# Loading four token tiles, a three-row rotation table and a last tile stored in two pieces: one change to a fused S5 and GEGLU kernel

## The chip, the cores and the metric

The kernel runs on one core of one Trainium2 chip. Its time is the device time of a whole execution in microseconds (us), the median of three runs; lower is better. A profiled execution gives besides the span, which is the stretch from the first to the last recorded instruction, and the time of each instruction in it.

## The reference

Input x is one sequence of 2048 tokens with 512 features, in bf16. The output is x plus the product of two branches of its layer norm:

```python
xn  = layernorm(x)                                    # 2048 x 512
Lam_bar = exp(dt * Lam);  B_bar = ((Lam_bar - 1) / Lam)[:, None] * B   # complex, 512 states
h_t = Lam_bar * h_(t-1) + B_bar @ xn_t                # over all 2048 tokens
s   = 2 * real(h @ C.T) + xn * Dskip
g   = silu((gelu(xn @ w_gate) * (xn @ w_up)) @ w_down)  # 512 -> 1376 -> 512
out = x + s * g
```

## The kernel before

**Tiling.** The 2048 tokens are four slabs of 512, and a slab is four row tiles of 128 tokens. Per slab the kernel normalises x, transposes it (`xnT`), multiplies it with the gate and up weights (1376 columns in chunks of 512, 512 and 352), multiplies the two results (`gated`), transposes that product by DMA (`at_t`, L549) and multiplies it with the down weight (`down_pair`, L562). Beside it, `half(s, h)` multiplies the slab with B for half of the states (L613), copies the result to a buffer `U` (L615), rotates it back by the angle of each token so that the complex recurrence becomes a real one, scans it (L644) and rotates it forward into `hst`. `y_part` (L573 to L587) multiplies `hst` with C (L577), starting from the skip term that ScalarE writes to the PSUM bank (L573), multiplies by the gate branch (L583), adds x (L584) and stores.

**The rotation.** `turn` multiplies `U` (or the scan's result `Fs`) with the tables in one instruction of 4096 elements per partition (`rot`, L625) into `Q`, and adds the two halves of `Q` (L637). The tables `tab` hold four rows: cosine, cosine again, sine and minus sine. The second cosine is copied by two DMAs, the last row by ScalarE. In slab 0 only rows 0 and 2 are read.

**The start of slab 0.** There is no transposed input yet, so TensorE transposes the tiles itself: `center(m)` subtracts the mean of tile m (ScalarE's sum at L421, VectorE's subtraction at L422), `head_t(m)` transposes it into a bank (L385, L398) and VectorE copies it out (L400) to `xcT`. The up weights come row tile by row tile (128 of the 512 features each), and `up_rows(m, k, c)` is one matmul of 512 columns for token tile m, weight row tile k and chunk c (L460), so that work can begin before all rows are there. Chunk 2 of up (352 columns) and all of gate follow by `first_w` (L497). Only then do slab 1 and later slabs go through `gate_tile` (L534), with `xnT` written by a DMA transpose (`dma_t4`, L434).

**What sets the order.** Each piece of work is a step in a plan: its engine, a function that emits it, what it reads and writes. `Plan.run` emits the steps in the order of a long tuple `ORDER`, written out as numbers. `SLOTS` says in the same way which buffer each group of a rotating pool takes, and `SIZES` how many the pool has: `ps` (six PSUM banks), `pp` (two), `U` and so on. So each engine does its steps in the order in which they stand in `ORDER`, and waits by semaphores. The cost and due-time arguments of the steps play no part at run time. All large transfers are issued from one queue, SP's; three small loads of parameters are issued by ScalarE's. The steps are numbered as they are created, and a step added early shifts all later numbers.

The emitted queue of SP begins: token tiles 0, 1 and 2 of slab 0; chunk 0 and chunk 1 of up row 0; up rows 1 and 2; token tile 3; up row 3; the last 352 columns of up; columns 512 to 1375 of gate; its first 512 columns; slab 1; `Drow`; then the DMA transposes of slab 0 and of B.

Of the kernel before, what the change touches and what calls it, by code (L numbers as in the profile page):

```python
# [10 lines left out]
AF = mybir.ActivationFunctionType  # L11
ALU = mybir.AluOpType
# [39 lines left out]
    ),  # L52
    "pp": (
        0, 0, 1, 0, 1, 0, 0, 1, 0, 1, 1, 0, 0, 0, 1, 0, 1, 0, 1, 0, 1, 1, 0, 1, 0, 1, 0, 0, 1, 0, 1, 0, 1, 1, 0, 0, 0, 1, 1,
    ),
    "U": (
        1, 0, 2, 1, 0, 2, 1, 0,
    ),
    "g2": (
        2, 1, 0, 5, 4, 2, 0, 3, 1, 0, 5, 3, 4, 2, 1, 5,  # L60
    ),
    "at": (
        3, 0, 2, 1, 3, 1, 2, 0, 0, 3, 2, 1, 2, 0, 1, 0,
    ),
    "gtA": (
        0, 1, 1, 0, 0, 0, 1, 1, 1, 1, 0, 1, 0, 1, 0, 1,
    ),
    "gtB": (
        0, 0, 1, 1, 1, 0, 1, 0, 0, 0, 1, 0, 0, 0, 1, 0,
    ),  # L70
    "ubA": (
        0, 0, 1, 1, 1, 0, 1, 0, 0, 1, 0, 1,
    ),
    "ubB": (
        1, 0, 1, 1, 0, 0, 1, 0, 0, 1, 0, 1,
    ),
    "yg": (
        0, 1, 0, 0, 1, 1, 1, 1, 0, 1, 0, 0, 1, 0, 1, 1, 1, 0,
    ),
    "ot": (  # L80
        0, 0, 1, 1, 1, 1, 0, 1, 1, 0, 0, 0, 1, 0, 1, 1, 0,
    ),
    "sk": (
        1, 0, 3, 2, 6, 4, 7, 5, 3, 2, 1, 0, 4, 7, 6, 5,
    ),
    "atT": (
        1, 0, 2, 3, 1, 2, 0, 2, 1, 3, 3, 2, 1, 0, 0, 2,
# [4 lines left out]
SIZES = {"ps": 6, "pp": 2, "U": 3, "g2": 6, "at": 4, "gtA": 2, "gtB": 2, "ubA": 2, "ubB": 2, "yg": 2, "ot": 2, "sk": 8, "atT": 4}  # L92
# [56 lines left out]
def kernel(  # L149
# [17 lines left out]
    nc = tc.nc  # L167
# [28 lines left out]
    def sb(name, shape, dt=BF16):  # L196
        return consts.tile(shape, dt, name=name)
# [20 lines left out]
    NU = 3  # L218
# [5 lines left out]
    tab = sb("tab", [P, 4, NPT, TS])  # L224
# [28 lines left out]
    def dve(n, emit, reads=(), writes=(), rate=1.0, base=DV, **kw):  # L253
        return pl.add(DVE, base + n / 960.0 / rate, emit, reads, writes, lag=0.13, **kw)
# [312 lines left out]
    def y_part(s, m, c0, c1):  # L567
# [7 lines left out]
        def f():  # L575
# [6 lines left out]
        go, io = pl.group("ot")  # L582
        dve(w, lambda: V.tensor_tensor(out=yg[iy][:, 0:w], in0=ps, in1=g2[ig][:, c0:c1], op=ALU.mult), [key, ("g2", gg)], [("yg", gy)])  # L583
        dve(w, lambda: V.tensor_tensor(out=ot[io][:, 0:w], in0=yg[iy][:, 0:w], in1=x_tok[:, s * M + m, c0:c1], op=ALU.add),  # L584
            [("yg", gy), ("x", s, m)], [("ot", go)], rate=2.0)
        mg = s * TS + m * P
        dma(SP, 0.35, 1.5, lambda: nc.sync.dma_start(out=out_td[mg : mg + P, c0:c1], in_=ot[io][:, 0:w]), [("ot", go)], [("out", s, m, c0)], svc=(2, 0.4, 0.9))  # L587

    def y_tile(s, m):
        cuts = (0, HD, D) if (s, m) == (NS - 1, M - 1) else (0, D)  # L590
        for c0, c1 in zip(cuts, cuts[1:]):
            y_part(s, m, c0, c1)
# [8 lines left out]
    TABS = ["tab0", "tab10", "tab11", "tab2", "tab3"]  # L601
    CTS = [("CT", 0), ("CT", 1)]

    def half(s, h):
# [17 lines left out]
        tf = tab[:, :, hs, :].rearrange("p (j r) q t -> p j r (q t)", j=2)  # L622
# [5 lines left out]
        def turn(src, dst, reads, writes, back):  # L628
            if s == 0:
                rot(src, tf[:, :, 0, :].unsqueeze(2).to_broadcast(WQ), reads + ["tab0", "tab2"])  # L630
                for ri in range(2):
                    op = ALU.add if (ri == 0) == back else ALU.subtract
                    dve(1024, lambda ri=ri, op=op: V.tensor_tensor(out=dst[:, ri, :], in0=Qf[:, 0, ri, :], in1=Qf[:, 1, 1 - ri, :], op=op),
                        ["Q"], writes, rate=2.0)
            else:
                rot(src, tf[:, :, ::-1, :] if back else tf, reads + TABS)
                dve(2048, lambda: V.tensor_tensor(out=dst, in0=Qf[:, 0, :, :], in1=Qf[:, 1, ::-1, :], op=ALU.add), ["Q"], writes, rate=2.0)  # L637
# [51 lines left out]
    def tables():  # L689
# [19 lines left out]
        tt(tab[:, 0], t1, t2, ALU.subtract, ["Q1", "Q2"], ["tab0"])  # L709
        tt(v4(t1), highs[1], lows[0], ALU.mult, ["sp", "ch"], ["Q1"])  # L710
        tt(v4(t2), highs[0], lows[1], ALU.mult, ["cp", "sh"], ["Q2"])
        tt(tab[:, 2], t1, t2, ALU.add, ["Q1", "Q2"], ["tab2", "Q"])
        for h in range(2):
            hp = slice(h * H2, (h + 1) * H2)
            dma(SP, 0.5, 2.0, lambda hp=hp: nc.sync.dma_start(out=tab[:, 1, hp, :], in_=tab[:, 0, hp, :]), ["tab0"], [f"tab1{h}"], svc=(2, 0.8, 1.0))
        acts(2048, lambda: act(out=tab[:, 3], in_=tab[:, 2], func=AF.Copy, scale=-1.0), ["tab2"], ["tab3"])
# [203 lines left out]
```

## Time and profile before

| | |
|---|---|
| three runs, median (lowest to highest) | 178.75 us (178.42 to 178.96) |
| the profiled execution's own time | 179.15 us |
| its span | 177.3 us |
| granted TensorE clock | 1.00 |
| instructions | 2411 |
| TensorE (PE) busy | 172.1 us, 97% |
| VectorE (DVE) busy | 155.6 us, 88% |
| ScalarE (ACT) busy | 131.4 us, 74% |
| GpSimd (POOL) busy | 11.9 us, 7% |

The page is one profiled execution. In its rows a group of instructions stands as engine, line of the kernel, operation, output <- input, with the shape of one and how many there are; x17 means 17 of them. A timeline row starts with the start and the length in microseconds, counted from the start of the span; what stands in brackets at its end is idle time before it and what ended it. The chain of waits follows the work that ended last back through what released each step. PE busy is the time in which TensorE has a matmul, and PEld its weight loads, which overlap it. Queue rows (SPq) show when the issuing engine wrote a transfer's descriptors, not when the data moved; the time to landing is in the DMA view.

### The profile page before, as it was taken

To read this page: it belongs to the slowest core of one execution; us is meant where nothing else is said; L and a number is where in the kernel's file an instruction comes from. 1 tells how busy PE (TensorE), PEld (TensorE's weight loads), DVE (VectorE), ACT (ScalarE), POOL (GpSimd) and SP (SyncE) were. 2 spreads that over 40 slices of the span, in tenths; PEclk is the share of its full clock that TensorE was granted. 3 is DMA by queue.
4 is the path that set the end of the run, shared out by engine and by line. 5 is a ranking of instruction groups with operands and counts; after the bars stand their busy time and mean duration, and the time that the engine had idled before them with its cause. 6 is when DMAs were issued, how large, how long until landed. Compare 5 with 4: busy or idle time off the path is not lost.

```text
span 177.3 us, 2411 instructions
## 1 busy us (share of the span) xinstructions
PE 172.1 (97%) x834; PEld 82.2 (46%) x849; DVE 155.6 (88%) x253; ACT 131.4 (74%) x245; POOL 11.9 (7%) x25
## 2 busy tenths in 40 slices
PE   8999999999999999999999999999999999999992
PEld 2455444454544444444454545454444444444451
DVE  3745799999889999899999999999999998999343
ACT  6779999989999999994749854685577866159210
POOL 1553300000002001300000000000000000000000
PEclk9999999999999999999999999999999999999999
DMA  5999999999914400600450431800500940320421
GB/s 153 286 357 228 149 255 215 274 234 234 201 37 81 81 0 4 118 0 0 77 117 4 89 90 59 163 0 4 111 0 0 204 99 4 73 67 30 83 89 59
DMA packets 48467, 19.19 MB, mean 108 GB/s; under 512 B 40296, under 2 KB 47816, under 8 KB 48456
## 3 DMA queue, kind: packets, MB, share of 16 engines
q1 hardware_dynamic: 48432, 19.04, 48.8%
q8 instruction: 6, 0.10, 0.2%
q14 instruction: 5, 0.04, 0.1%
q10 hardware_dynamic: 24, 0.00, 0.0%
HBM read 6.46 MB, written 2.10 MB: 48 GB/s over the span
## 4 chain that ended last, share of the span: by engine, by line
PE 80%; DMA 12%; ACT 3%; SPq 2%; issue 1%; DVE 0%; ACTq 0%
PE bank L534 31%; PE bank L562 21%; PE bank L577 16%; PE bank L613 12%; DMA xnT<-xna 7%; DMA x_tok<-in_A_x_dram 5%; ACT xna L843 2%; SPq L287 1%; ACT gtA L503 1%; ACT at L469 1%; SPq L296 1%; DVE yg L583 0%; DVE ot L584 0%; ACT gtB L503 0%; ACTq L843 0%
## 5 line engine op out<-in xcount | busy, mean ns | idle before, releaser
L534 PEld LDWEIGHTS <-xnT 128*128 128x128 bf16 x288 | 28.1, 98 | 29.5 <-DMA xnT<-xna 0.6
L562 PE MATMUL bank<-wd,atT 128*128 128x512 bf16 (+1 forms) x171 | 39.4, 379 | 0.3
L534 PE MATMUL bank<-wu,xnT 128*128 128x512 bf16 (+1 forms) x142 | 32.5, 357 | 0.1
L534 PE MATMUL bank<-wg,xnT 128*128 128x512 bf16 (+1 forms) x139 | 31.7, 356 | 0.4
L613 PE MATMUL bank<-xnT,BT 128*128 128x512 bf16 x128 | 31.7, 379 | 0.0
L644 DVE TENSOR_TENSOR_SCAN Fs<-rho,ini,W 128x512 bf16<-128x512 f32 x24 | 29.9, 1272 | 0.1
L577 PE MATMUL bank<-C,hst 128*128 128x512 bf16 (+1 forms) x135 | 29.1, 367 | 0.1
L562 PEld LDWEIGHTS <-atT 128*128 128x128 bf16 (+1 forms) x176 | 17.2, 98 | 20.4
L615 ACT ACTIVATE U<-bank 128x512 bf16<-128x512 f32 x32 | 18.5, 611 | 6.3 <-PE bank L613 6.3
L565 ACT ACTIVATE g<-bank 128x512 f32<-128x512 f32 x16 | 9.5, 596 | 14.7 <-PE bank L562 14.6
L537 ACT ACTIVATE ubA<-bank 128x512 bf16<-128x512 f32 x24 | 14.6, 609 | 7.4 <-PE bank L534 5.4
L577 PEld LDWEIGHTS <-hst 128*128 128x128 bf16 x136 | 13.3, 98 | 14.2
L613 PEld LDWEIGHTS <-BT 128*128 128x128 bf16 x128 | 12.4, 98 | 14.4 <-DMA BT<-in_A_B_re_dram 0.4
L625 DVE TENSOR_TENSOR Q<-U,tab 128x4096 bf16<-128x4096 bf16 x8 | 18.3, 2290 | 0.5
L625 DVE TENSOR_TENSOR Q<-Fs,tab 128x4096 bf16<-128x4096 bf16 x8 | 18.3, 2289 | 0.2
L583 DVE TENSOR_TENSOR yg<-bank,g 128x512 bf16<-128x512 f32 (+1 forms) x17 | 11.0, 656 | 7.1 <-PE bank L577 6.6
L537 ACT ACTIVATE gtA<-bank 128x512 bf16<-128x512 f32 x24 | 14.5, 609 | 1.8 <-PE bank L534 1.5
L838 ACT ACTIVATE junk<-x_tok 128x512 bf16<-128x512 bf16 x16 | 10.3, 660 | 0.0
L573 ACT ACTIVATE bank<-sk 128x512 f32<-128x512 bf16 (+1 forms) x17 | 9.9, 590 | 0.1
L497 PE MATMUL bank<-wg,W 128*128 128x512 bf16 (+1 forms) x47 | 9.9, 357 | 0.1
L644 DVE TENSOR_TENSOR_SCAN Fs<-rho,W 128x512 bf16<-128x512 f32 x8 | 9.5, 1211 | 0.0
L843 ACT ACTIVATE xna<-x_tok,nb,rs 128x512 bf16<-128x512 bf16 x12 | 9.3, 826 | 0.0
(120 smaller groups left out, 185.1 us busy)
## 6 DMA issues: line engine op xcount, KB each, us to landing
out_dram<-ot SPq DMA_DIRECT2D x15, 128.0 KB, 1.7
x_tok<-in_A_x_dram SPq DMA_DIRECT2D x3, 512.0 KB, 6.2
wd<-in_B_w_down_dram SPq DMA_DIRECT2D x1, 1280.0 KB, 6.9
wg<-in_B_w_gate_dram SPq DMA_DIRECT2D x1, 864.0 KB
wu<-in_B_w_up_dram SPq DMA_DIRECT2D x3, 256.0 KB, 4.0
x_tok<-in_A_x_dram SPq DMA_DIRECT2D x4, 128.0 KB, 2.4
wg<-in_B_w_gate_dram SPq DMA_DIRECT2D x1, 512.0 KB, 7.9
tab<-tab SPq DMA_DIRECT2D x2, 256.0 KB, 7.1
```

The costliest lines, as they stand in the source:

```text
L497: T.matmul(ps[:, 0 : b - a], lhsT=xcT[:, k, m * P : (m + 1) * P], rhs=wt[:, k, a:b], start=(k == 0), stop=(k == KT - 1))
L534: T.matmul(ps[:, 0 : b - a], lhsT=xnT[:, s % 2, m, k, :], rhs=wt[:, k, a:b], start=(k == 0), stop=(k == KT - 1))
L537: acts(b - a, lambda: act(out=dst, in_=ps[:, 0 : b - a], func=AF.Copy if up else AF.Gelu_apprx_tanh), [key], [ok], table=None if up else " ...
L562: T.matmul(ps[:], lhsT=atT[:fs, k, iT * P : (iT + 1) * P], rhs=wd[:fs, k, :], start=(k == 0), stop=(k == NFT - 1))
L577: T.matmul(ps, lhsT=hst[s % 2][:, j // NPT, j % NPT, m * P : (m + 1) * P], rhs=C2[:, j // NPT, j % NPT, c0:c1], start=False, stop=(j == 2 ...
L583: dve(w, lambda: V.tensor_tensor(out=yg[iy][:, 0:w], in0=ps, in1=g2[ig][:, c0:c1], op=ALU.mult), [key, ("g2", gg)], [("yg", gy)])
L613: T.matmul(ps[:], lhsT=BT[:, ri, k, pt * P : (pt + 1) * P], rhs=xnT[:, s % 2, :, k, :], start=(k == 0), stop=(k == KT - 1))
L615: acts(512, lambda q=q, ri=ri, ps=ps: act(out=U[ui][:, ri, q, :], in_=ps[:], func=AF.Copy), [key], [("U", ug, q, ri)])
L625: dve(4096, lambda: V.tensor_tensor(out=Qf, in0=src.unsqueeze(1).to_broadcast(WQ), in1=table, op=ALU.mult), reads, ["Q"], rate=2.0)
L644: pl.add(DVE, 1.12 if s == 0 else 1.185, lambda ri=ri, q=q, pt=pt, first=first: V.tensor_tensor_scan(out=Fs[:, ri, q, :], data0=rho[:, pt ...
L838: acts(512, lambda i=i, fn=fn, sc=sc, m=m: act(out=junk()[:], in_=x_tok[:, s * M + m, :], func=fn, scale=sc, accum_out=sx[:, s, i, m : m + ...
L843: acts(512, lambda m=m: act(out=xn[m], in_=x_tok[:, s * M + m, :], func=AF.Identity, scale=rs[:, s, m : m + 1], bias=nb[:, s, m : m + 1]), ...
```

## The change

**Loads.** Rows 1 and 2 of the up weights are loaded in halves, chunk 0 and chunk 1 apart, as row 0 is. The order of creation of the load steps is tiles 0, 1, 2, row 0, row 1, tile 3, row 2, row 3 and so on; the emitted order is that of `ORDER`, and there SP's queue begins: tiles 0, 1, 2; chunks 0 and 1 of row 0; chunks 1 and 0 of row 1; chunks 0 and 1 of row 2; token tile 3; row 3; the last columns of up; the gate weights; slab 1; `Drow`.

**Tables.** `tab` has three rows, minus sine, cosine and sine. The two copies of the cosine are gone. Slabs 1 to 3 read the table through an access pattern that names overlapping windows of two neighbouring rows; the layout of `Q` follows, and the halves to be added are its other axis. There are four `U` buffers in place of three.

**The last token tile of y** is computed in three parts of 160, 160 and 192 columns, in place of two of 256. The first two share one output buffer and one store of 320 columns.

**Order.** `ORDER` and `SLOTS` are new throughout. In TensorE's queue the transposes of tile 3 stand behind 13 of the row products (18 before). One B product of slab 0 moves behind the start of slab 1. The first two pairs of down products and the B products of slab 2 come earlier in the queue. The transposed load of B's imaginary half stands ahead of slab 0's `xnT` in SP's queue, and both C transposes ahead of `w_down`.

```diff
 SLOTS: "ps", "pp", "U", "g2", "at", ... all new
-SIZES = {"ps": 6, "pp": 2, "U": 3, ...}
+SIZES = {"ps": 6, "pp": 2, "U": 4, ...}
-    NU = 3
+    NU = 4
-    tab = sb("tab", [P, 4, NPT, TS])
+    tab = sb("tab", [P, 3, NPT, TS])
...
     load_w("wu", 0, 1, W1, W2, 3.0, 4.95)
-    load_w("wu", 1, 2, 0, W2, 3.94, 6.05)
+    load_w("wu", 1, 2, 0, W1, 3.47, 5.5)
+    load_w("wu", 1, 2, W1, W2, 3.94, 6.05)
     load_x(3, 4.41, 6.6)
-    load_w("wu", 2, 3, 0, W2, 5.35, 7.7)
+    load_w("wu", 2, 3, 0, W1, 4.88, 7.15)
+    load_w("wu", 2, 3, W1, W2, 5.35, 7.7)
...
-    def y_part(s, m, c0, c1):
+    def y_part(s, m, c0, c1, begin=None, more=False):
...
-        go, io = pl.group("ot")
+        go, io = begin[1] if begin else pl.group("ot")
+        b0 = begin[0] if begin else c0
...
+        if more:
+            return b0, (go, io)
-        dma(SP, 0.35, 1.5, lambda: nc.sync.dma_start(out=out_td[mg : mg + P, c0:c1], in_=ot[io][:, 0:w]), ...
+        dma(SP, 0.35, 1.5, lambda: nc.sync.dma_start(out=out_td[mg : mg + P, b0:c1], in_=ot[io][:, 0 : c1 - b0]), ...
...
     def y_tile(s, m):
-        cuts = (0, HD, D) if (s, m) == (NS - 1, M - 1) else (0, D)
-        for c0, c1 in zip(cuts, cuts[1:]):
-            y_part(s, m, c0, c1)
+        if (s, m) != (NS - 1, M - 1):
+            y_part(s, m, 0, D)
+            return
+        y_part(s, m, 160, 320, begin=y_part(s, m, 0, 160, more=True))
+        y_part(s, m, 320, D)
...
-        tf = tab[:, :, hs, :].rearrange("p (j r) q t -> p j r (q t)", j=2)
+        tf = tab[:, :, hs, :].rearrange("p z q t -> p z (q t)")
+
+        def windows(back):
+            z = tf.ap[1][0]
+            d = z if back else -z
+            return bass.AP(tensor=tf.tensor, offset=tf.offset + z, ap=[list(tf.ap[0]), [d, 2], [-d, 2], list(tf.ap[2])])
...
-                rot(src, tf[:, :, ::-1, :] if back else tf, reads + TABS)
-                dve(2048, lambda: V.tensor_tensor(out=dst, in0=Qf[:, 0, :, :], in1=Qf[:, 1, ::-1, :], op=ALU.add), ["Q"], writes, rate=2.0)
+                rot(src, windows(not back), reads + TABS)
+                dve(2048, lambda: V.tensor_tensor(out=dst, in0=Qf[:, :, 0, :], in1=Qf[:, :, 1, :], op=ALU.add), ["Q"], writes, rate=2.0)
...
-        for h in range(2):
-            hp = slice(h * H2, (h + 1) * H2)
-            dma(SP, 0.5, 2.0, lambda hp=hp: nc.sync.dma_start(out=tab[:, 1, hp, :], in_=tab[:, 0, hp, :]), ["tab0"], [f"tab1{h}"], svc=(2, 0.8, 1.0))
-        acts(2048, lambda: act(out=tab[:, 3], in_=tab[:, 2], func=AF.Copy, scale=-1.0), ["tab2"], ["tab3"])
+        acts(2048, lambda: act(out=tab[:, 0], in_=tab[:, 2], func=AF.Copy, scale=-1.0), ["sin"], ["nsin"])
```

More of the change, by code (lines that the diff above doesn't have):

```diff
@@ L48 @@
     "ps": (
[3 rows of a table removed]
[3 rows of a table added]
     ),
     "pp": (
-        0, 0, 1, 0, 1, 0, 0, 1, 0, 1, 1, 0, 0, 0, 1, 0, 1, 0, 1, 0, 1, 1, 0, 1, 0, 1, 0, 0, 1, 0, 1, 0, 1, 1, 0, 0, 0, 1, 1,
+        0, 0, 1, 0, 1, 0, 1, 0, 1, 1, 0, 0, 1, 0, 1, 0, 0, 0, 1, 1, 0, 1, 1, 0, 1, 1, 0, 1, 0, 0, 1, 1, 0, 0, 1, 1, 1, 1, 0,
     ),
     "U": (
-        1, 0, 2, 1, 0, 2, 1, 0,
+        0, 1, 3, 2, 0, 1, 2, 3,
     ),
     "g2": (
-        2, 1, 0, 5, 4, 2, 0, 3, 1, 0, 5, 3, 4, 2, 1, 5,
+        3, 0, 2, 1, 4, 1, 2, 5, 5, 3, 4, 0, 1, 0, 2, 3,
     ),
     "at": (
-        3, 0, 2, 1, 3, 1, 2, 0, 0, 3, 2, 1, 2, 0, 1, 0,
+        2, 1, 3, 0, 1, 0, 2, 3, 0, 1, 2, 3, 0, 1, 3, 2,
     ),
     "gtA": (
-        0, 1, 1, 0, 0, 0, 1, 1, 1, 1, 0, 1, 0, 1, 0, 1,
+        0, 1, 0, 1, 1, 0, 1, 0, 0, 0, 1, 1, 1, 1, 1, 0,
     ),
     "gtB": (
-        0, 0, 1, 1, 1, 0, 1, 0, 0, 0, 1, 0, 0, 0, 1, 0,
+        0, 1, 1, 0, 0, 0, 1, 1, 1, 0, 1, 0, 1, 1, 0, 0,
     ),
     "ubA": (
-        0, 0, 1, 1, 1, 0, 1, 0, 0, 1, 0, 1,
+        0, 1, 0, 1, 0, 1, 1, 0, 1, 1, 0, 0,
     ),
     "ubB": (
-        1, 0, 1, 1, 0, 0, 1, 0, 0, 1, 0, 1,
+        0, 0, 1, 1, 1, 0, 1, 1, 0, 1, 1, 0,
     ),
     "yg": (
-        0, 1, 0, 0, 1, 1, 1, 1, 0, 1, 0, 0, 1, 0, 1, 1, 1, 0,
+        0, 1, 1, 1, 0, 1, 1, 0, 0, 1, 1, 0, 0, 0, 0, 0, 1, 0, 1,
     ),
     "ot": (
-        0, 0, 1, 1, 1, 1, 0, 1, 1, 0, 0, 0, 1, 0, 1, 1, 0,
+        1, 1, 0, 1, 0, 1, 0, 1, 1, 0, 0, 1, 0, 0, 1, 1, 0,
     ),
     "sk": (
-        1, 0, 3, 2, 6, 4, 7, 5, 3, 2, 1, 0, 4, 7, 6, 5,
+        0, 2, 3, 1, 6, 7, 4, 5, 2, 0, 1, 3, 6, 5, 7, 4,
     ),
     "atT": (
-        1, 0, 2, 3, 1, 2, 0, 2, 1, 3, 3, 2, 1, 0, 0, 2,
+        3, 0, 1, 2, 0, 2, 3, 1, 1, 3, 2, 0, 0, 2, 3, 1,
     ),
 }
-SIZES = {"ps": 6, "pp": 2, "U": 3, "g2": 6, "at": 4, "gtA": 2, "gtB": 2, "ubA": 2, "ubB": 2, "yg": 2, "ot": 2, "sk": 8, "atT": 4}
+SIZES = {"ps": 6, "pp": 2, "U": 4, "g2": 6, "at": 4, "gtA": 2, "gtB": 2, "ubA": 2, "ubB": 2, "yg": 2, "ot": 2, "sk": 8, "atT": 4}
 class Plan:
@@ L581, in y_part @@
         gy, iy = pl.group("yg")
-        go, io = pl.group("ot")
+        go, io = begin[1] if begin else pl.group("ot")
+        b0 = begin[0] if begin else c0
         dve(w, lambda: V.tensor_tensor(out=yg[iy][:, 0:w], in0=ps, in1=g2[ig][:, c0:c1], op=ALU.mult), [key, ("g2", gg)], [("yg", gy)])
-        dve(w, lambda: V.tensor_tensor(out=ot[io][:, 0:w], in0=yg[iy][:, 0:w], in1=x_tok[:, s * M + m, c0:c1], op=ALU.add),
-            [("yg", gy), ("x", s, m)], [("ot", go)], rate=2.0)
+        dve(w, lambda: V.tensor_tensor(out=ot[io][:, c0 - b0 : c1 - b0], in0=yg[iy][:, 0:w], in1=x_tok[:, s * M + m, c0:c1], op=ALU.add),
+            [("yg", gy), ("x", s, m)], [("ot", go, c0)], rate=2.0)
+        if more:
+            return b0, (go, io)
         mg = s * TS + m * P
-        dma(SP, 0.35, 1.5, lambda: nc.sync.dma_start(out=out_td[mg : mg + P, c0:c1], in_=ot[io][:, 0:w]), [("ot", go)], [("out", s, m, c0)], svc=(2, 0.4, 0.9))
+        dma(SP, 0.35, 1.5, lambda: nc.sync.dma_start(out=out_td[mg : mg + P, b0:c1], in_=ot[io][:, 0 : c1 - b0]),
+            [("ot", go, b0), ("ot", go, c0)], [("out", s, m, b0)], svc=(2, 0.4, 0.9))
     def y_tile(s, m):
-        cuts = (0, HD, D) if (s, m) == (NS - 1, M - 1) else (0, D)
-        for c0, c1 in zip(cuts, cuts[1:]):
-            y_part(s, m, c0, c1)
+        if (s, m) != (NS - 1, M - 1):
[3 more added lines that the diff above has]
+        y_part(s, m, 320, D)
     ini = [sb(f"ini{h}", [P, 2, H2], FP32) for h in range(2)]
@@ L599 @@
     cS, sS = cbt[:, :, NBA - 1], sbt[:, :, NBA - 1]
-    TABS = ["tab0", "tab10", "tab11", "tab2", "tab3"]
+    TABS = ["nsin", "cos", "sin"]
     CTS = [("CT", 0), ("CT", 1)]
@@ L629, in turn @@
             if s == 0:
-                rot(src, tf[:, :, 0, :].unsqueeze(2).to_broadcast(WQ), reads + ["tab0", "tab2"])
+                rot(src, tf[:, 1:3, :].unsqueeze(2).to_broadcast(WQ), reads + ["cos", "sin"])
                 for ri in range(2):
@@ L708, in tables @@
         tt(v4(t2), highs[1], lows[1], ALU.mult, ["sp", "sh"], ["Q2"])
-        tt(tab[:, 0], t1, t2, ALU.subtract, ["Q1", "Q2"], ["tab0"])
+        tt(tab[:, 1], t1, t2, ALU.subtract, ["Q1", "Q2"], ["cos"])
         tt(v4(t1), highs[1], lows[0], ALU.mult, ["sp", "ch"], ["Q1"])
         tt(v4(t2), highs[0], lows[1], ALU.mult, ["cp", "sh"], ["Q2"])
-        tt(tab[:, 2], t1, t2, ALU.add, ["Q1", "Q2"], ["tab2", "Q"])
-        for h in range(2):
-            hp = slice(h * H2, (h + 1) * H2)
-            dma(SP, 0.5, 2.0, lambda hp=hp: nc.sync.dma_start(out=tab[:, 1, hp, :], in_=tab[:, 0, hp, :]), ["tab0"], [f"tab1{h}"], svc=(2, 0.8, 1.0))
-        acts(2048, lambda: act(out=tab[:, 3], in_=tab[:, 2], func=AF.Copy, scale=-1.0), ["tab2"], ["tab3"])
+        tt(tab[:, 2], t1, t2, ALU.add, ["Q1", "Q2"], ["sin", "Q"])
+        acts(2048, lambda: act(out=tab[:, 0], in_=tab[:, 2], func=AF.Copy, scale=-1.0), ["sin"], ["nsin"])
     dummies(7)
```

54 rows, old and new, of tables (ORDER, SLOTS) are left out of this document.

## The prediction, made before the changed kernel had run

> **What bounds the kernel now.** I read the page's busy shares and its chain first, then a table of five stretches, then the chain in order of time and each engine's timeline at the two ends of the span. A row of the stretches has the stretch, its length, TensorE's busy time and matmuls, the granted clock, the share of the DMA engines and GB/s.
>
> ```profile
> span 177.3 us, 2411 instructions
> PE 172.1 (97%) x834; PEld 82.2 (46%) x849; DVE 155.6 (88%) x253; ACT 131.4 (74%) x245; POOL 11.9 (7%) x25
> PE 80%; DMA 12%; ACT 3%; SPq 2%; issue 1%; DVE 0%; ACTq 0%
> ```
>
> ```profile
> 0.00:3.84 3.84, 3.08 (x8) 1.00 0.46 132
> 3.84:5.83 1.99, 1.53 (x17) 1.00 0.96 290
> 5.83:31.80 25.97, 25.77 (x132) 1.00 1.06 245
> 31.80:174.20 142.40, 141.68 (x683) 1.00 0.39 82
> 174.20:177.30 3.10, 0.00 (x0) 1.00 0.15 42
> ```
>
> TensorE bounds it: 97% busy at clock 1.00, and from 5.83 to 174.20 it stands still for under a microsecond in all. VectorE at 88% is next, but nothing waits for it there. So the body offers nothing to win: the change touches no matmul of it, and a new order can only keep TensorE as full or make a hole. What can be won lies ahead of 5.83, in one short wait near 31.8, and behind 174.2. What can be lost is any hole that the new order makes.
>
> ```profile
> 1.65 2.69 DMA x_tok<-in_A_x_dram
> ...
> 26.35 5.41 DMA xnT<-xna
> ...
> 71.74 4.32 PE bank L577 x20
> ```
>
> The chain begins with the landing of token tile 2 (1.65 + 2.69 = 4.34) and is TensorE's nearly all the way after 31.8. Its last row gives the pace: 4.32 / 20 = 0.216 us for a matmul of 512 columns.
>
> **The front: where tile 3 is met.** The words say that all four token tiles come ahead of the up weights. The emitted order of SP's queue does not: it is tiles 0, 1, 2, then six half rows of the up weights (rows 0, 1, 2), then tile 3. Before, it is tiles 0, 1, 2, two halves of row 0, rows 1 and 2 whole, then tile 3: the same bytes ahead of tile 3, in two more transfers. On TensorE, though, tile 3's four transposes now stand after 13 of the row products (L462), where 18 (L460) stood ahead of them.
>
> ```profile
> 5.59 0.40 PE L398 MATMUL bank<-ident,xna 128*128 128x128 bf16 x4 [0.29 <-DVE xna L422]
> 5.83 3.95 PE L460 MATMUL bank<-wu,W 128*128 128x512 bf16 x17
> 9.61 0.39 PE L398 MATMUL bank<-ident,xna 128*128 128x128 bf16 x4
> 9.84 1.89 PE L460 MATMUL bank<-wu,W 128*128 128x512 bf16 x7
> ```
>
> ```profile
> 0.72 1.35 SPq L296 DMA_DIRECT2D x_tok<-in_A_x_dram  x3
> 2.12 1.86 SPq L287 DMA_DIRECT2D wu<-in_B_w_up_dram  x4
> 4.36 0.33 SPq L296 DMA_DIRECT2D x_tok<-in_A_x_dram  x1
> 5.68 1.06 SPq L287 DMA_DIRECT2D wg<-in_B_w_gate_dram  x2
> ```
>
> SP issues a transfer every 0.47 us (1.40 / 3 up to 2.12). Four from 2.12 would end at 4.00, yet tile 3 goes at 4.36, just after tile 2's landing at 4.34; tile 2 is the transfer eight places back (three small ones of ACT counted), and I read this as a wait for a shared semaphore. In the new order the same place is the first half of row 2; it goes at 4.36, the second half at 4.73, and tile 3 at 5.20, 0.84 later than now.
>
> ```profile
> DMA to landing us min/median/max: 2.2/2.4/3.7
> ```
>
> ```profile
> wg<-in_B_w_gate_dram SPq DMA_DIRECT2D x1, 512.0 KB, 7.9
> ...
> wu<-in_B_w_up_dram SPq DMA_DIRECT2D x2, 128.0 KB, 2.5
> ```
>
> ```profile
> 8.10 0.63 ACT L421 ACTIVATE junk<-x_tok 128x512 bf16<-128x512 bf16 x1 [0.97 <-DMA x_tok<-in_A_x_dram]
> ```
>
> ```profile
> 8.86 0.35 DVE L422 TENSOR_SCALAR xna<-x_tok,ma 128x512 bf16<-128x512 bf16 x1
> ```
>
> The first of these rows is for the four token tiles: tile 3 was the slowest, 4.36 + 3.7 = 8.0, among whole rows. In the new order one 128 KB transfer goes each 0.47 us, and such ones landed after 2.5; tile 3 then lands at 5.20 + 2.5 = 7.7. The bounds are 5.20 + 2.2 = 7.4, and 8.3 if the queue is as full as now. From landing to TensorE it takes 1.25 (ACT's sum at 8.10, the subtraction at 8.86 for 0.35, 0.06 to TensorE as from L422 to 5.59), so TensorE can go on at 8.95. It arrives at 5.83 + 12 x 0.216 = 8.42 (one of the 13 products stands ahead of 5.83) and waits 0.53; everything behind on TensorE waits with it. After the transposes (0.23, from 9.61 to 9.84) it is 9.18, with five products (1.08) still owed: 10.26 against 9.84 now. **Term: +0.42**, from -0.11 (no wait) to +1.02 (8.3).
>
> By the Trainium skill (DMA: Bandwidth & Descriptors, section Anatomy of one DMA) a transfer takes a fixed 2.0 us and its bytes at 436 GB/s, fitted on the GpSimd path; that makes an estimate of 2.3 us for 128 KB, a landing at 7.5 and a term of +0.22. The row's 2.5 decides.
>
> What the halves save, a wait for row 1 hidden in the 3.95 (17 x 0.216 = 3.67 against 3.78 from 5.83 to 9.61: 0.11), now lies ahead of the wait for tile 3 and is worth nothing. The last gate transfer (512 KB) is issued about 6.2 and takes 7.9: 14.1; issued 0.9 later, it lands at 15.0. TensorE needs those columns behind 19 row products (4.1), a gate product (4 x 0.216) and four tail products of 4 x 0.149 (352/512 of 0.216), so at 9.18 + 7.3 = 16.5. The cover is 1.5 and I cost it at nothing; were it gone, TensorE would stand for what lands behind 16.5.
>
> **The wait for slab 1's transposed rows.**
>
> ```profile
> 29.81 1.89 PE L613 MATMUL bank<-xnT,BT 128*128 128x512 bf16 x8
> 31.80 0.77 PE L534 MATMUL bank<-wg,xnT 128*128 128x352 bf16 x4
> ```
>
> Eight matmuls from 29.81 end at 31.54; TensorE then waits 0.26 for the transfer that lands at 26.35 + 5.41 = 31.76. In the new order one product of B (0.86) moves from ahead of this point to behind it, so TensorE arrives at 31.54 - 0.86 + 0.42 = 31.10. ACT's queue ahead of the last normalisation holds the same up and gate evictions, and the other slab load that shared the queue now comes later, so the landing is between 30.3 and 32.0. **Term: -0.10**, from -0.26 (no wait) to +0.64. In this range SP's moved transposes count: BT's imaginary half goes ahead of slab 0's xnT, and both C transposes ahead of w_down.
>
> **The tables.** Two 256 KB copies go, and the ACT negation stays under another name.
>
> ```profile
> tab<-tab SPq DMA_DIRECT2D x2, 256.0 KB, 7.1
> ```
>
> ```profile
> L625 DVE TENSOR_TENSOR Q<-U,tab 128x4096 bf16<-128x4096 bf16 x8 | 18.3, 2290 | 0.5
> L625 DVE TENSOR_TENSOR Q<-Fs,tab 128x4096 bf16<-128x4096 bf16 x8 | 18.3, 2289 | 0.2
> ```
>
> The copies are not in the chain: 0. The rotation now reads an overlapping window of three tables. Now, reading them reversed (Q<-U) or forward (Q<-Fs) costs the same, 2290 and 2289 ns, so I take 0; below nothing is excluded, the instruction being no smaller. The fourth U buffer ends no wait that I see: 0.
>
> **The tail.**
>
> ```profile
> 174.20 0.42 DVE L583 TENSOR_TENSOR yg<-bank,g 128x256 bf16<-128x256 f32 x1
> 174.66 0.29 DVE L584 TENSOR_TENSOR ot<-yg,x_tok 128x256 bf16<-128x256 bf16 x1
> ```
>
> Behind the last matmul now stand 192 columns, not 256: 0.71 becomes 0.53 if in proportion, 0.71 if fixed. I take half the difference, and 0.03 for a store of 48 KB, not 64: **-0.12**, from -0.21 to 0. The second part's work, in proportion to 160 of 256 columns 0.44, fits under the last part's eight matmuls (8 x 0.216 x 192/512 = 0.65).
>
> **Sum.** +0.42 - 0.10 - 0.12 = +0.20. The profiled execution took 179.15 (1.85 more than its span); the sum makes it 179.35. The median is 178.75, 0.40 less; the prediction is 178.95. A measurement of this kernel can tell about 0.3%, 0.54 us, from no change.
>
> **Rivals.** *Tile 3 as late as now (0.17).* Six small transfers ahead of it gain nothing and it lands at 8.1 or later: terms +0.82 to +1.02, the sum +0.6 to +0.8, 179.45. For it: tile 3 was the slowest of four. Against it, two stretches (columns as above, without TensorE's):
>
> ```profile
> 2.50:4.50 2.00, 1.00 0.98 264
> 4.50:6.50 2.00, 1.00 0.92 274
> ```
>
> The queue moves as much in the stretch of small transfers as in that of whole rows. The Trainium skill's rule (same page, Rules for kernel authors) speaks for this rival: join small transfers into large ones, a megabyte or more for full bandwidth; these two rows differ by 4%.
>
> *The first down product waits (0.19; slower).* The new order has it 17 steps after slab 1's rows are needed (13 x 0.864 + 4 x 0.596 = 13.6), near 44.8.
>
> ```profile
> 31.33 2.29 DVE L625 TENSOR_TENSOR Q<-U,tab 128x4096 bf16<-128x4096 bf16 x1
> ```
>
> ```profile
> L644 DVE TENSOR_TENSOR_SCAN Fs<-rho,W 128x512 bf16<-128x512 f32 x8 | 9.5, 1211 | 0.0
> ```
>
> ```profile
> 39.65 5.17 SPq L549 DMA_TRANSPOSE atT<-at  x3
> ```
>
> ```profile
> atT<-at SPq DMA_TRANSPOSE x16, 3.6
> ```
>
> Now the first gate transpose is issued at 39.65. In the new order tile 1's gate is complete behind a rotation (2.29), four scans of 1.21 and what I estimate at 2 of sums, products and small work: about 9 us after the first rotation starts, so at 40.3; with 3.6 to land, 43.9. From 0.9 us later on, TensorE stands still; w_down, now issued behind two C transposes, shares that moment. Price 0.4 to 2.0: 179.35 to 181.
>
> *The window halves VectorE's rate (0.02).* Twelve rotations with 2.2 us more are 26 us, over VectorE's 12% of idle time (21 us): 184 or more.
>
> *Tile 3 early (0.12).* It lands by 7.2, nothing waits for it, nor for slab 1: -0.11 - 0.26 - 0.20 = -0.57: 178.2.
>
> **How the numbers follow.** Forecast 0.50, all within 0.3%; of the early case 0.10 is faster by more, 0.02 not; the late tile, the down product and the window are slower: 0.38. So faster 0.10, same 0.52, slower 0.38. The range from 178.2 to 180.6 takes in the early case, the late tile and most of the down product's. The forecast's own is 178.4 to 179.25.
>
> **What would show it.** Right: SP issues tile 3 near 5.2, TensorE idles about 0.5 us before the second group of transposes at 8.4 to 9.0, no idle near 31.5, and matmuls at 0.216 from there. Wrong: a hole over 0.3 us anywhere from 32 to 170, rotations longer than 2.3 us, tile 3 landing before 7.3 or after 8.2.

## The result and the profile after

The changed kernel takes 179.57 us (median of 11 runs, 178.97 to 180.87); the kernel before, run beside it, 178.54 (11 runs, 178.20 to 179.16). The ratio is 1.0054, with a 95% interval from 1.0035 to 1.0074: slower by about 0.96 us (0.6 to 1.3). The profiled execution took 180.34, on the upper side of its runs, as that of before did (179.15 among 178.20 to 179.16); its span is 1.22 us longer (178.56 against 177.34).

The page first, then TensorE's busy time in stretches that were cut at its two waits (stretch, length, TensorE busy and matmuls, granted clock, share of the DMA engines, GB/s).

```profile
span 178.6 us, 2449 instructions
PE 173.3 (97%) x857; PEld 82.9 (46%) x857; DVE 155.1 (87%) x255; ACT 131.1 (73%) x246; POOL 11.1 (6%) x25
PE 82%; ACT 8%; DMA 5%; SPq 2%; issue 1%; DVE 1%; ACTq 0%
```

```profile
6.00:8.54 2.54, 2.54 (x15) 1.00 0.94 273
8.54:9.81 1.27, 0.17 (x2) 1.00 0.99 268
9.81:31.65 21.84, 21.84 (x114) 1.00 1.01 220
31.65:32.30 0.65, 0.39 (x3) 1.00 0.48 89
32.30:175.36 143.06, 143.06 (x708) 1.00 0.38 81
```

TensorE still bounds the kernel. From 32.30 to its last matmul it is busy without a gap. It stands still only ahead of that, in two holes. ScalarE now holds 8% of the chain, where it held 3%.

The first hole, on TensorE's timeline, and what stands ahead of it: SP's queue, the landings of the four token tiles, and ScalarE.

```profile
5.95 2.75 PE L462 MATMUL bank<-wu,W 128*128 128x512 bf16 x12
9.81 0.40 PE L400 MATMUL bank<-ident,xna 128*128 128x128 bf16 x4 [1.10 <-DVE xna L424]
```

```profile
2.11 2.82 SPq L287 DMA_DIRECT2D wu<-in_B_w_up_dram  x6
4.97 0.43 SPq L296 DMA_DIRECT2D x_tok<-in_A_x_dram  x1
```

```profile
DMA to landing us min/median/max: 2.2/2.2/3.6
```

```profile
8.64 0.63 ACT L423 ACTIVATE junk<-x_tok 128x512 bf16<-128x512 bf16 x1 [2.81 <-DMA x_tok<-in_A_x_dram]
```

Tile 3 is issued at 4.97 and lands at 8.56. ScalarE's sum over it starts at 8.64, and TensorE's transposes at 9.81, 1.25 after the landing. The twelve products ahead end at 8.54 (5.95 + 12 x 0.216), so TensorE stands still for 1.27 us. ScalarE stood for 2.81 us with that sum at the head of its queue. This cost it less than it seems: its first eviction (its first copy of an up product out of a bank) waits again, for TensorE, and is ended by the row products behind tile 3's transposes:

```profile
12.89 0.69 ACT L471 ACTIVATE at<-bank,rs 128x512 bf16<-128x512 f32 x1 [0.62 <-PE bank L462]
```

The second hole is the wait for slab 1, on the chain of waits and on the timeline:

```profile
12.89 5.94 ACT at L471 x11
...
24.17 2.80 ACT xna L853 x4
...
26.99 5.25 DMA xnT<-xna
```

```profile
32.29 1.04 PE L536 MATMUL bank<-wu,xnT 128*128 128x512 bf16 x4 [0.26 <-DMA xnT<-xna]
```

ScalarE's evictions begin at 12.89, and by the chain its queue is on the path from there until slab 1's normalised rows are done; their transpose is issued at 26.99 (26.35 before) and lands at 32.24. By the starts of the matmuls the hole is 0.42, where before had 0.27.

This hole goes with the 5.25 us that the transpose took to land in this one execution, and with 5.41 in the profile of before. In the eleven other profiles below whose landing can be told it took 4.4 to 4.9, and none of them waits more than 0.05 for slab 1. One of them (the run with ScalarE freed, below) has tile 3 as late as here and issues the transpose at the same moment. Its issue, its landing and TensorE's first products with slab 1:

```profile
26.98 1.79 SPq L436 DMA_TRANSPOSE xnT<-xna  x1
```

```profile
DMA to landing us min/median/max: 4.4/4.4/4.4
```

```profile
31.79 1.46 PE L536 MATMUL bank<-wu,xnT 128*128 128x512 bf16 x5
```

It lands at 31.39, and TensorE goes on to slab 1 at 31.79 without a wait; in the changed kernel it arrives at 31.87. So the wait for slab 1 is not shown to belong to the change. Why the transpose took longer in two of the profiles is open.

The tail and the rotation:

```profile
175.57 0.36 DVE L586 TENSOR_TENSOR yg<-bank,g 128x192 bf16<-128x192 f32 x1
175.96 0.26 DVE L587 TENSOR_TENSOR ot<-yg,x_tok 128x192 bf16<-128x192 bf16 x1
```

```profile
L638 DVE TENSOR_TENSOR Q<-U,tab 128x4096 bf16<-128x4096 bf16 x8 | 18.3, 2290 | 1.1 <-ACT U L623 0.8
L638 DVE TENSOR_TENSOR Q<-Fs,tab 128x4096 bf16<-128x4096 bf16 x8 | 18.3, 2286 | 0.1
```

**The sum over the two profiled spans.** The group of products behind tile 2's transposes begins at 5.95 in place of 5.83: +0.12. TensorE's holes behind it, taken from the starts of its matmuls, are 1.27 + 0.42 = 1.69 in place of 0.27 + 0.11 + 0.08 = 0.46: +1.23. From the last matmul's end (its start and its columns at the pace of 0.216 for 512) to the end of the span it is 0.15 less. Together +1.20, of 1.22 measured. The matmuls themselves are the same: the last matmul's end less that start and less the holes is 167.7 in both, and in every run below but one. The start of that group moves by more than 0.12 from one execution to the next (5.36 to 6.08 below), and slab 1's wait is open, so what the sum puts down to the change is 1.27 - 0.11 - 0.15 = 1.01; by the ratio of the runs it costs about 0.96.

### The profile page after: what moved, and what is told of

Read it like the earlier page. It is cut to its first block, busy times and chain, and to the rows that moved or that the text cites. A ratio compares the mean times of both kernels' runs of the same rounds, so it can differ in the third digit from the quotient of the medians.

```text
span 178.6 us, 2449 instructions
## 1 busy us (share of the span) xinstructions
PE 173.3 (97%) x857; PEld 82.9 (46%) x857; DVE 155.1 (87%) x255; ACT 131.1 (73%) x246; POOL 11.1 (6%) x25
## 4 chain that ended last, share of the span: by engine, by line
PE 82%; ACT 8%; DMA 5%; SPq 2%; issue 1%; DVE 1%; ACTq 0%
PE bank L536 31%; PE bank L564 21%; PE bank L579 16%; PE bank L621 12%; ACT at L471 4%; DMA xnT<-xna 3%; DMA x_tok<-in_A_x_dram 2%; ACT xna L853 2%; ACT gtA L505 2%; PE bank L462 1%; SPq L287 1%; ACT L505 1%; SPq L296 1%; ACT junk L423 0%; ACT gtB L505 0%
## 5 line engine op out<-in xcount | busy, mean ns | idle before, releaser
L536 PE MATMUL bank<-wu,xnT 128*128 128x512 bf16 (+1 forms) x144 | 32.0, 357 | 0.3 <-DMA xnT<-xna 0.3
L536 PE MATMUL bank<-wg,xnT 128*128 128x512 bf16 (+1 forms) x144 | 31.5, 357 | 0.0
L621 PE MATMUL bank<-xnT,BT 128*128 128x512 bf16 x128 | 31.1, 379 | 0.0
L579 PE MATMUL bank<-C,hst 128*128 128x512 bf16 (+2 forms) x144 | 29.8, 355 | 0.0
L623 ACT ACTIVATE U<-bank 128x512 bf16<-128x512 f32 x32 | 18.8, 620 | 5.7 <-PE bank L621 5.6
L638 DVE TENSOR_TENSOR Q<-U,tab 128x4096 bf16<-128x4096 bf16 x8 | 18.3, 2290 | 1.1 <-ACT U L623 0.8
L638 DVE TENSOR_TENSOR Q<-Fs,tab 128x4096 bf16<-128x4096 bf16 x8 | 18.3, 2286 | 0.1
L586 DVE TENSOR_TENSOR yg<-bank,g 128x512 bf16<-128x512 f32 (+2 forms) x18 | 11.3, 626 | 3.5 <-ACT g L567 2.1
L575 ACT ACTIVATE bank<-sk 128x512 f32<-128x512 bf16 (+2 forms) x18 | 10.1, 565 | 0.1
L518 DVE TENSOR_TENSOR at<-gtA,ubA 128x1024 bf16<-128x1024 bf16 x12 | 8.2, 685 | 1.9 <-ACT ubA L539 1.4
```

What stands on the lines that cost most here:

```text
L536: T.matmul(ps[:, 0 : b - a], lhsT=xnT[:, s % 2, m, k, :], rhs=wt[:, k, a:b], start=(k == 0), stop=(k == KT - 1))
L575: acts(w, lambda: act(out=ps, in_=skt[:, c0:c1], func=AF.Copy), [kk], [key])
L579: T.matmul(ps, lhsT=hst[s % 2][:, j // NPT, j % NPT, m * P : (m + 1) * P], rhs=C2[:, j // NPT, j % NPT, c0:c1], start=False, stop=(j == 2 ...
L621: T.matmul(ps[:], lhsT=BT[:, ri, k, pt * P : (pt + 1) * P], rhs=xnT[:, s % 2, :, k, :], start=(k == 0), stop=(k == KT - 1))
L623: acts(512, lambda q=q, ri=ri, ps=ps: act(out=U[ui][:, ri, q, :], in_=ps[:], func=AF.Copy), [key], [("U", ug, q, ri)])
L638: dve(4096, lambda: V.tensor_tensor(out=Qf, in0=src.unsqueeze(1).to_broadcast(WQ), in1=table, op=ALU.mult), reads, ["Q"], rate=2.0)
```

## Experiments

All times are medians beside runs of the kernel before on the same chip (178.8 to 178.9 there); ratios are to it, are taken over all runs with a 95% interval, and can differ by up to 0.2% from the ratio of the two medians. "The changed kernel" is 1.0054.

**Tile 3 really ahead of the weights.** One number moves in `ORDER`, so that SP issues tile 3 fourth:

```diff
- ..., 0, 1, 2, 25, 3, 26, 4, 27, 30, 44, 6, 5, 8, 9, 7, 10, ...
+ ..., 0, 1, 2, 25, 7, 3, 26, 4, 27, 30, 44, 6, 5, 8, 9, 10, ...
```

> The changed kernel with one step moved: SP issues token tile 3 fourth, ahead of all up weights. Theory of the front: TensorE stood still for 1.27 us before tile 3's transposes, which landed at 8.56; issued at about 2.2 it lands before 5, the wait goes, and the first weights come 0.45 later, which may cost up to 0.4 at about 5.2. Expected 0.9 to 1.3 us less than the changed kernel, 178.3 to 178.7. Rival, the full queue: whatever comes last in it is late by the same amount, and the rows of the weights now make TensorE wait: 0 to 0.4 us less than the changed kernel.

Measured: 178.79, ratio 0.9994 (0.9968 to 1.0021). Set against 1.0054 that is 0.6% or 1.07 us less than the changed kernel. SP's and TensorE's timelines:

```profile
0.72 1.83 SPq L296 DMA_DIRECT2D x_tok<-in_A_x_dram  x4
```

```profile
5.74 2.75 PE L462 MATMUL bank<-wu,W 128*128 128x512 bf16 x12
8.33 0.39 PE L400 MATMUL bank<-ident,xna 128*128 128x128 bf16 x4
```

5.74 + 12 x 0.216 = 8.33: no hole. The wait for slab 1 is gone too. Its transpose is issued at 25.52, 1.47 sooner, but TensorE arrives 1.46 sooner as well (30.41 for 31.87); what ends the wait is that the transpose takes 4.5 us to land and not 5.25, with which there would be one of about 0.4. The theory of the front holds, the rival of the full queue fails: the weights that now come 0.45 later make nothing wait.

**Tile 3 eighth**, behind rows 0 and 1 and ahead of row 2 (the 7 moved ahead of the 8).

> The changed kernel with tile 3 eighth in SP's queue, behind both halves of rows 0 and 1 and ahead of row 2, in place of tenth. Issued at about 4.0, with 2.4 to 3.5 to land it is there at 6.4 to 7.5 and on TensorE at 7.7 to 8.8, which arrives at 8.3 to 8.4. Theory of the late tile: a wait of 0 to 0.5 us in place of 1.27, none for slab 1, 0.9 to 1.5 us less than the changed kernel. Rival, that anything issued ahead of 128 KB transfers makes room only for itself: row 2's products wait as long as tile 3 did, and the gain is under 0.4.

Measured: 178.70, ratio 0.9991 (0.9979 to 1.0002), 1.1 us less than the changed kernel, as the theory of the late tile said.

```profile
4.03 0.43 SPq L296 DMA_DIRECT2D x_tok<-in_A_x_dram  x1
```

```profile
DMA to landing us min/median/max: 2.1/2.2/2.7
```

It lands at 6.73 and no hole follows, nor one for slab 1; one of 0.12 near 22.0 is left. Two places earlier are enough.

**Tile 3 twelfth**, behind all up weights.

> The changed kernel with tile 3 twelfth in SP's queue, behind the whole of the up weights, in place of tenth: the suspected cost made larger. Issued 0.95 us later and behind 256 + 352 KB more. Theory of the late tile: the wait ahead of its transposes grows from 1.27 to 2.2 us at least (2.2 by the issue alone, up to 3.5 if it also waits behind the bytes), the wait for slab 1 stays near 0.4, and the time is 0.9 to 2.2 us above the changed kernel, 180.5 to 181.8. Rival, that tile 3 in the changed kernel lands late whatever its place, because the queue is full to 8 us: no change beyond 0.3.

Measured: 183.83, ratio 1.0273 (1.0254 to 1.0292), 3.9 us above the changed kernel and far outside what was expected. The timeline, the landings and two stretches:

```profile
11.72 0.61 PE L400 MATMUL bank<-ident,xna 128*128 128x128 bf16 x4 [3.53 <-DVE xna L424]
```

```profile
DMA to landing us min/median/max: 2.1/2.2/4.5
```

```profile
7.80:11.70 3.90, 0.39 (x2) 0.98 1.00 303
11.70:15.00 3.30, 3.28 (x11) 0.51 1.17 377
```

The hole is 3.70, 2.43 more than in the changed kernel, and a little over the 3.5 that also waiting behind the bytes allowed. But then TensorE runs at half its clock for some 3 us: 0.51 in the row, and products at 0.427 in place of 0.216. Seven of them cost 1.4 us more and the transposes ahead of them 0.2, which no expectation had priced. In the two profiled spans it is +2.43 + 1.6, less 0.42 for slab 1's wait and 0.51 for products that begin at 5.44: 3.1, of 3.05 between the spans. The wait for slab 1, which was to stay, is gone although ScalarE stood 4.9 us at tile 3. The Trainium skill (TensorE: Matmul & The Clock Gate, Part 1) says that after an idle window of about 3.4 us the clock falls to half and that a busy one brings it back; this run agrees, with a hole of 3.70 and a slow stretch of about 3, while the hole of 1.27 in the changed kernel kept the clock at 1.00.

**The five products back ahead of tile 3 on TensorE**, SP's queue as changed; four row-3 products moved behind the transposes.

```diff
 # TensorE's steps only (81: tile 3's transposes; 89, 91, ...: its products)
- 83, 85, 81, 88, 74, 87, 86, 89, 91, 97, 90, ..., 84, 105, ...
+ 83, 85, 88, 74, 87, 86, 84, 81, 97, 105, 95, 99, 89, 91, 90, ...
```

> The changed kernel with SP's queue as it is, and on TensorE five row products of tiles 0 to 2 moved ahead of tile 3's transposes (18 ahead of them, as in the kernel before) and four products with row 3 behind them, to cover the copy of tile 3 out of its bank. Theory of the place in TensorE's queue: five products are 5 x 0.216 = 1.08 us, so the wait falls from 1.27 to 0.2 and the time by 1.1 us, to 178.5. Theory of the later landing (the six small transfers alone made the loss): the wait stays above 0.8 and the time falls by 0.3 at most.

Measured: 179.49, ratio 1.0018 (0.9992 to 1.0045). By the ratios that is 0.6 us below the changed kernel, but the two intervals overlap: not told apart.

```profile
9.71 0.40 PE L400 MATMUL bank<-ident,xna 128*128 128x128 bf16 x4 [0.27 <-DVE xna L424]
9.95 2.75 PE L462 MATMUL bank<-wu,W 128*128 128x512 bf16 x12
13.36 0.76 PE L499 MATMUL bank<-wu,W 128*128 128x352 bf16 x4 [0.66 <-ACT at L471]
```

The wait for tile 3 falls to 0.44, near the 0.2 of the theory of the place, but 0.83 stands again at 12.3: together 1.27, just what it was. The products that fill the first wait had covered the eviction of tile 3's bank, which the first product of 352 columns needs: 12 products stand between tile 3's transposes and that one, where the changed kernel has 17. What this profile gains, slab 1's wait and a start of the products at 5.58, are the two terms that vary between executions. Neither theory came true: the place was right for the first wait and overlooked the second.

**ScalarE freed of tile 3's sum**, on top of that run (`ORDER`: tile 2's squares, the angles and the two sines ahead of steps 48 and 49, tile 2's scale ahead of tile 3's).

> The run in which 18 products stand ahead of tile 3's transposes on TensorE, and besides, on ScalarE, VectorE and GpSimd, what does not need tile 3 (tile 2's squares, the two sines with the angles ahead of them, tile 2's scale) is moved ahead of tile 3's sum, which waits 2.7 us for its landing. Theory of the second path (ScalarE stands behind tile 3's sum, and its evictions start 1.5 us late and hold the bank that TensorE needs at 12.3): the second wait of 0.83 us falls under 0.2, the first stays at 0.3 to 0.6, and the time is 0.6 us below that run, at about the kernel before. Rival, that TensorE's banks are held by the number of evictions and not by when they start: the wait stays above 0.6 and the time as it was.

Measured: 179.71, ratio 1.0050 (1.0034 to 1.0066); no gain. The theory of the second path falls here:

```profile
12.89 3.31 ACT L471 ACTIVATE at<-bank,rs 128x512 bf16<-128x512 f32 x6 [2.07 <-PE bank L462]
```

ScalarE is ready 2 us sooner and waits for TensorE; the second hole is 0.79. By this wait, what sets it is the distance in TensorE's own queue from the products behind tile 3's transposes to the next user of a bank of theirs, which the moved products had made short; no run varies that distance alone. Moving these products does not hide a late tile 3: they are wanted on both sides of it.

**The B product put back ahead of slab 1** (step 198 and its copy 199 ahead of 311).

> The changed kernel with the B product of slab 0 that it had moved behind the start of slab 1 put back ahead of it (its copy by ScalarE too). Theory that slab 1's wait is set by ScalarE's normalisation and the transposing DMA alone: the wait of 0.42 us near 31.7 is filled with 0.86 us of work that has to be done anyway, and the time falls by 0.4, to 179.15. Rival, that the copy or the product shifts the chain that slab 1's rows hang on: no change, the wait stays at 0.4.

Measured: 180.10, ratio 1.0064 (1.0043 to 1.0084); the rival's outcome in the time, no gain.

```profile
34.55 1.67 PE L621 MATMUL bank<-xnT,BT 128*128 128x512 bf16 x7 [0.26 <-ACT U L623]
```

The wait for slab 1 is filled, and a hole of 0.42 stands two products later, where TensorE waits for a copy by ScalarE (L623). So here ScalarE is the late one.

**The halves alone**, in the kernel before, with the changed kernel's order of SP's loads.

> The kernel before with nothing but the halved loads of rows 1 and 2, in the order in which the changed kernel issues them; TensorE's order is that of before, 18 products ahead of tile 3's transposes. Theory of the place in TensorE's queue: tile 3 lands at 8.3 to 8.6 in place of 8.02, and of that 0.3 to 0.4 is covered: 0 to 0.3 us more than the kernel before, 178.5 to 178.9. Theory of the later landing: the loss is here, 0.8 to 1.1 us more, 179.4 to 179.6.

Measured: 179.30, ratio 1.0016 (0.9993 to 1.0039): 0.3 us above the kernel before, from 0.1 below to 0.7 above. That is the upper end of the theory of the place and below the 0.8 of the other.

```profile
5.94 3.93 PE L462 MATMUL bank<-wu,W 128*128 128x512 bf16 x17
9.71 0.39 PE L400 MATMUL bank<-ident,xna 128*128 128x128 bf16 x4
```

Tile 3 lands as late as in the changed kernel (issued 4.97, 3.5 to land: 8.46), and TensorE reaches its transposes at 9.71 without a wait, though with nothing to spare (8.46 + 1.25 = 9.71). The place of its transposes on TensorE is what makes the landing cost 1.27. There is no wait for slab 1 here either, with tile 3 late.

**Tile 3 fourth in the order of before** (with the halves).

> The kernel before with the halved rows and tile 3 fourth on SP, ahead of all up weights; every other engine's order, the tables and the tail are those of before. Theory that tile 3 had cover enough in the order of before: nothing is gained at tile 3, the rows come 0.45 later with the first products, and the time is that of the kernel before within 0.3 us. Rival, that an early tile 3 frees ScalarE and VectorE sooner and so slab 1's rows: the wait of 0.27 near 31.5 goes, 0.3 to 0.5 us less.

Measured: 179.34, ratio 1.0045 (1.0022 to 1.0068): both expectations missed.

```profile
6.08 4.00 PE L462 MATMUL bank<-wu,W 128*128 128x512 bf16 x17
```

Seventeen products take 3.83 in this row up to 9.91, 0.16 more than 3.67: a wait for a row that comes later now; they begin at 6.08. Slab 1's wait is gone as the rival said, but not for its reason: it is gone in the run with the halves alone too. The span is 177.53 against 177.34, and 0.26 us more than before lies behind VectorE's last sum; that makes up for the wait at slab 1, and why the time is 0.4 to 1.2 us longer over its runs is open.

**Whole rows with tile 3 between them**, in the changed kernel.

> The changed kernel with rows 1 and 2 of the up weights loaded whole again and tile 3 between them: the same 896 KB stand ahead of it as in the run with tile 3 eighth, but in one transfer fewer, so SP issues it about 0.5 us sooner, near 3.55. Theory of the bytes (a full queue moves some 250 GB/s and a transfer lands when the bytes ahead of it have passed): it lands at 6.4 to 6.9 as in that run, at 6.73. Theory of the place (a landing is the issue and about 2.4 us): it lands near 6.0. Either way nothing waits for it, and the time is that of the run with tile 3 eighth within 0.2 us, 178.6 to 178.9.

Measured: 179.12, ratio 1.0033 (1.0008 to 1.0059).

```profile
3.55 0.44 SPq L296 DMA_DIRECT2D x_tok<-in_A_x_dram  x1
```

```profile
DMA to landing us min/median/max: 2.1/2.3/3.2
```

```profile
8.36 0.59 PE L460 MATMUL bank<-wu,W 128*128 128x512 bf16 x2 [0.21 <-DMA wu<-in_B_w_up_dram]
```

3.55 + 3.2 = 6.75: issued half a microsecond sooner, tile 3 lands at the same moment as behind the same bytes in halves (6.73). The theory of the bytes holds against that of the place. That nothing waits was wrong: row 2 comes whole and late, and TensorE has a hole of 0.38 for it. So here the halves are worth about 0.4 us, once tile 3 is out of the way.

**The tail in two parts**, with tile 3 fourth.

> The run with tile 3 fourth, and the last token tile of y in two parts of 256 columns, as before the change. Theory: the end of the span stands 3.30 us behind the last matmul in place of 3.23, and the time is 0.1 us more, which is at the edge of what can be told. Rival, that one more part is worth its larger share: 0.3 us more. Rival, that three parts cost as much as they save: no difference behind the last matmul.

Measured: 178.71, ratio 0.9992 (0.9980 to 1.0003); not told apart from three parts (0.9994). Behind the end of the last matmul the spans of three-part kernels end 3.19 to 3.34 us later (nine of them), and those of two parts 3.34 to 3.60 (five).

**The three-row table alone**, in the kernel before.

> The kernel before with nothing but the three-row table read by windows, without the two copies. Theory that neither the copies nor the access pattern is on the path: rotations at 2.29 us as before, the time that of the kernel before within 0.2 us. Rival, that overlapping windows slow VectorE or that the copies' 7 us on the DMA queues delayed a load: over 0.3 us to either side.

Measured: 178.92, ratio 0.9999 (0.9985 to 1.0012).

```profile
L630 DVE TENSOR_TENSOR Q<-U,tab 128x4096 bf16<-128x4096 bf16 x8 | 18.3, 2289 | 0.5
L630 DVE TENSOR_TENSOR Q<-Fs,tab 128x4096 bf16<-128x4096 bf16 x8 | 18.3, 2288 | 0.2
```

Nothing either way, as expected.

**One more matmul ahead of the data**, with tile 3 eighth (`dummies(8)`).

> The run with tile 3 eighth, and one more of the matmuls that keep TensorE busy ahead of the first data (8 in place of 7, the last one from 3.7 to 4.15). Theory of the slow start: matmuls of 512 columns take 0.427 us until 4.5 to 6.0 and 0.216 from there, a busier TensorE passes sooner from the one to the other, and the first products start up to 0.4 us earlier: 178.3 to 178.6. Rival, that the moment of passing has nothing to do with one matmul more: within 0.1 us of that run, 178.6 to 178.8, or slower by up to 0.2 since the transposes of the parameters wait for it.

Measured: 179.09, ratio 1.0004 (0.9983 to 1.0025): the rival in its reason, and slower than it allowed (by the medians 0.39 above the run with tile 3 eighth, by the ratios 0.2). TensorE passed to full speed at 5.4, within the spread of the other runs, and the parameters' transposes began at 4.26 in place of 3.84.

No run beats the kernel before clearly. The best, tile 3 eighth, is 0.9991 (0.9979 to 1.0002), and TensorE has 0.12 us of holes left in it behind 5.4.

## Why the prediction was right or wrong

The time lies in the range, but the likeliest case did not happen. It was the first rival, "tile 3 as late as now", in mechanism and nearly in size: it gave 179.45, 179.57 was measured. The forecast's own range ended at 179.25, and a change of +0.20 was forecast where about +0.96 was measured; that the whole range held is owed to the room it left for the slower rivals. By the prediction's own signs, a landing after 8.2 and a wait near 31.5 spoke against it.

- **Where tile 3 is met: right.** It was the tenth transfer, 13 products stood ahead of its transposes, TensorE reached them at 8.54 (8.42 forecast), and 1.25 us from landing to TensorE came out at 1.25.
- **When it lands: the step that failed.** The forecast was 5.20 + 2.5 = 7.7, with 8.3 as its upper bound; it landed at 4.97 + 3.59 = 8.56. SP issued it at 4.97 and not at 5.20, for it had nothing to wait for: tile 2 had landed at 3.87. (The wait that the prediction read fits all profiles: the eighth transfer of SP never goes ahead of tile 2's landing, and follows it within 0.02 us where that is late.) The 2.5 was the wrong row: it is how long 128 KB took at the head of the queue. With the DMA engines busy at 0.9 and more, tile 3 landed the later, the more bytes stood ahead of it: 384 KB ahead, at 4.4 to 4.6; 896 KB, at 6.7 to 6.9; 1152 KB, at 7.9 and 8.0 in whole rows and 8.2 to 8.8 in halves; 1760 KB, at 10.5. From 896 to 1760 that is 864 KB in 3.7 us, about 240 GB/s. The moment of issue hardly counts: 3.55 or 4.03 gave 6.75 or 6.73, and 4.01 in the run with the tables alone gave 7.9, where 4.36 had given 8.0. The row with 3.7, which the prediction quoted for tile 3 itself, behind the same bytes, was the one to take: 8.02 at the least.
- **The term of the front** was thus +1.16 (1.27 for the wait, less the 0.11 of row 1), where +0.42 was taken and +1.02 was the upper end.
- **The small transfers.** That the queue moves as much in halves as in whole rows was read from two stretches of one profile, in which both kinds are under way. Three stretches of the kernel before with nothing but the halves changed (stretch, length, clock, DMA share, GB/s), and the third of the kernel before, whose first two the prediction shows:

```profile
2.50:4.50 2.00, 1.00 0.89 233
4.50:6.50 2.00, 1.00 0.91 255
6.50:8.50 2.00, 1.00 0.86 243
```

```profile
6.50:8.50 2.00, 1.00 0.95 286
```

  That is 1462 KB in the six microseconds (2 x 731), against 1648 (2 x 824). The other profiles of these two queues fit: 1676 KB in the run with the tables alone, which has SP's queue of before, and 1356 to 1590 in the four with that of the change. But the run with whole rows and tile 3 between them moved only 1478, so that the size of the transfers makes the difference is not shown. The Trainium skill's rule to join transfers (DMA: Bandwidth & Descriptors, Rules for kernel authors) spoke for the rival; the two queues agree with its direction, the run with whole rows does not. The Trainium skill's figure for one transfer (same page, Anatomy of one DMA), which gave 7.5, is further off than the row's.
- **Slab 1: not shown.** -0.10 was forecast, and the two profiles give +0.15 (0.42 against 0.27), inside its range. Both waits go with a transpose that took longer to land than in the other profiles (5.25 and 5.41 against 4.4 to 4.9), and with 4.8 there would be none in either. The step took the wait of the one profile for a property of the kernel.
- **The tail, -0.12:** -0.15 between the two profiles; in the medians two parts and three are not told apart. **The tables, 0:** 0.9999. **VectorE's rate by windows:** 2290 and 2286 ns, and that rival is out.
- **The first down product:** the other slower rival. It came at 45.91 in TensorE's queue and waited for nothing.
- **What is left of the halves' use:** "worth nothing" holds in the changed order, since their gain lies ahead of the wait for tile 3; with tile 3 out of the way they are worth the 0.38 us hole of the run with whole rows.

The cause is shown from two sides: with tile 3's load moved and nothing else, the loss goes (0.9994); with the same late load and the order of TensorE from before, the wait does not arise (1.0016). What the change's words say, all four token tiles ahead of the up weights, its `ORDER` did not do.

## What to carry to other kernels

In a queue that keeps the DMA engines busy, price a landing by the bytes ahead of it, not by the issue and the time that a transfer of its size took elsewhere; in these runs splitting what stood ahead moved nothing forward. Start from a landing that was measured behind known bytes and take the difference at the rate of the busy stretch. The rate alone is too early: when tile 3 landed in the changed kernel, 205 GB/s over 8.56 us, some 1750 KB, had been moved, and 1280 KB stood ahead of it and in it. Read the emitted order of the queue and not the order in which the loads are written. A load that comes late stops every engine that has its consumer at the head of the queue, but here only TensorE, which bounds the kernel, is shown to have paid: it lost 1.27 us, while no wait of the changed kernel is shown to come from ScalarE's 2.81. And a wait that stands in one profile may be that execution's alone: look for it in the profiles of kernels that have the same order there, before a term is built on it.

## What the runs showed of the hardware

TensorE starts slowly, and the profile's clock column does not show it: up to a moment that lies before 4.6 us of the span in one profile and near 6.5 in another, matmuls of 512 columns follow each other at 0.427 us, and then at 0.216, while the granted clock reads 1.00 all along. The moment differs from one execution to the next (with tile 3 eighth, the transposes from 4.57 on already follow each other at 0.06, where they take 0.11 at half speed; it is 4.7 before, 5.4 with tile 3 fourth and 5.8 after; with the tables alone a product at 6.01 still takes 0.41). The start of the products behind tile 2's transposes varies too, from 5.36 to 6.08, though not with that moment alone: with the tail in two parts TensorE was at full speed by 4.6 and they began at 5.95. That is as much as many an edit here is worth, and a reason not to read a single profile's span too finely. The Trainium skill (TensorE: Matmul & The Clock Gate, Part 1) says that the window which decides on the clock runs freely and that the point of passing therefore varies; that it varies agrees, and no run here shows the window. Only in the run with tile 3 twelfth, after 3.7 us without work, did the column show a drop between matmuls, to 0.51.
